# Attention with a learned bias and two MLP layers: query tiles moved to the outermost loop, heads taken two by two inside it

## The chip, the cores and the metric

The kernel runs on one core of a Trainium2 chip. The metric is the device time of one execution in microseconds (us); the time quoted for the kernel before is the median of 3 runs. A traced execution gives, beside its own time, a span from its first to its last instruction.

## What is computed

The reference works in float32 on a batch of 2, with 8 heads, a sequence of 576 and a head width of 64. Each score gets a bias that a small network computes from the distance of the two positions; the softmaxed scores weigh `v`; the result goes, token by token, through two gated MLP layers (hidden width 1536).

```python
scores = q @ k.T / sqrt(64)                               # B=2, H=8, S=576, D=64
x = log1p(abs(i - j)) / log1p(max(i, 1))                  # one number per (i, j)
bias = relu(x * w1 + b1) @ w2                             # 32 hidden units -> 8 heads
attn = softmax(scores + bias)
x = (attn @ v) as [1152 tokens, 512]
x = ((x @ w_a) * (x @ w_b)) @ w_out                       # first MLP, 512 -> 1536 -> 512
out = (silu(x @ w_gate) * (x @ w_val)) @ w2_out           # second MLP
```

## The kernel before

The 8 heads are handled as 4 pairs `p`. The 576 queries of a batch element are cut into tiles `t`: four of 128 rows (`t` = 0 to 3) and one of 64 (`t` = 4, for which the 64 rows of both batch elements share one tile of 128 partitions).

**Bias.** The bias depends on heads and positions, not on the batch, and is made once, in 36 units of 16 query rows for all heads. `Bias.make` runs four `hidden` operations (L122 on VectorE or L124 on ScalarE), fp32 matmuls (L146, 8 or 16 records each unit) and two to four scaling copies into a staging tile `bt` (L128, L130; `BTS` = 4 such tiles), which a DMA writes to a DRAM buffer `bias_d` (L159). A tile step reads its rows back (L349, or L353 and L354 into `pad` for `t` = 4). The first 12 units (`FIRST`) are made ahead of the first step, the others inside the first ten steps (`MADE`).

**Steps.** There are 20 steps (p, g, t). Group g = 0 holds the tiles 4, 0, 1 of a pair and g = 1 the tiles 2, 3. `Heads.load` fetches q of the group and the whole k of the pair for each (p, g), so that k is loaded and split into a high and a low part (`ka`, `kb`, L174 or L172 and L176) twice for each pair; `load_v` fetches v twice as well. Loads for the next (p, g) are put on SP's queue behind the bias reads of the current step. A step of a 128-row tile does, for each batch element b, one `scores` call: 12 matmuls into the four-bank PSUM tile `ps` (L256, one buffer), and for each head j a VectorE operation that adds the bias and finds the maximum (L259) and the exponential on ScalarE (L265). `es` is one tile for each head j with both batch elements side by side, from a ring of three. Then 18 transposes (L281) in groups of three go through a ring of three PSUM banks, each group copied to `ee` by VectorE or ScalarE (L271, L273, chosen by `Share`).

**Finish.** When the last tile of a (p, g) is done, `finish` turns the sums into reciprocals, spreads and transposes them (L295, L300, L303), multiplies `ee` with `v` for all 320 or 256 queries of one batch element at once (L312: 10 matmuls, each two records in the trace, into the one PSUM bank `pu`), scales (L314) and splits the result into `xh` and `xl` (L324, L325), the input of the MLPs.

**MLPs.** `moe` works on three chunks of 384 tokens. Its matmuls (L414) are 72 steps of 36. Weights come packed in pieces of 512 KB (`Weights.part`, L216 to L226); the first three pieces are asked for in step (2, 1, 2), the 17th of 20. The order of all instructions on each engine is set when the program is built, by a planner that goes by priorities in program order and its own costs.

Of the kernel before, what the change touches and what calls it, by code (L numbers as in the profile page):

```python
# [17 lines left out]
P = 128  # L18
# [10 lines left out]
QW = (704, 512)  # L29
LEFT = (512, 576)  # L30
TILES = ((4, 0, 1), (2, 3))
BW = 591
FAR = -1.0e30

UNITS = (*range(32, 36), *range(32))
FIRST = 12
MADE = (4, 4, 2, 2, 2, 2, 2, 2, 2, 2)
HDS, BTS = 8, 4
# [55 lines left out]
class Bias:  # L94
# [7 lines left out]
    def __init__(self, tc, stack, cst, lm, bias_d, heads, share):  # L102
# [15 lines left out]
        with tc.issue_after(ready.ins), tc.issue_after(last_load.ins):  # L118
            heads.load(0, 0)
# [12 lines left out]
    def make(self, u, banks):  # L132
# [9 lines left out]
        ps = [banks() for a in range(parts)]  # L142
        bt = self.bc.tile([P, BW], F32, tag="bt", name="bt", bufs=BTS)
        for a in range(parts):
            for cg in range(4):
                nc.tensor.matmul(ps[a][32 * cg : 32 * cg + 32, :w], self.W2, hd[cg][:, w * a : w * a + w], start=True, stop=True)  # L146
            if n == f:
                self.scaled(bt[:, z + w * a : z + w * a + w], ps[a][:, :w], w, u)
                c = min(z, w * a + w - 1) - max(w * a - 1, 0)
                if c > 0:  # L150
                    o = max(w * a - 1, 0)
                    self.scaled(bt[:, :z][:, ::-1][:, o : o + c], ps[a][:, 1 + o - w * a : 1 + o - w * a + c], c, u)
            else:
                self.scaled(bt[:, : z + 1][:, ::-1][:, w * a : w * a + w], ps[a][:, :w], w, u)
                c = min(f - 1, w * a + w - 1) - max(w * a - 1, 0)
                if c > 0:
                    o = max(w * a - 1, 0)
                    self.scaled(bt[:, z + 1 + o : z + 1 + o + c], ps[a][:, 1 + o - w * a : 1 + o - w * a + c], c, u)
# [3 lines left out]
class Heads:  # L162
# [5 lines left out]
    def split(self, raw, n, tags, bufs):  # L168
        hi, lo = (self.pool.tile([P, n[1]], F32R, tag=x, name=x, bufs=bufs) for x in tags)
        w = n[0]  # L170
        if self.share.on_dve(w, DFAST):
            self.nc.vector.tensor_copy(hi[:, :w], raw[:, :w])  # L172
        else:
            self.nc.scalar.copy(hi[:, :w], raw[:, :w])  # L174
        self.share.dve(w)
        self.nc.vector.tensor_tensor(lo[:, :w], raw[:, :w], hi[:, :w].bitcast(F32), op=ALU.subtract)  # L176
        return hi, lo

    def load(self, p, g):
        nc, n = self.nc, QW[g]  # L180
        raw = self.pool.tile([P, QW[0]], F32, tag="raw", name="raw", bufs=1)
        nc.sync.dma_start(raw[:, :n], self.d[0][p][:, g * QW[0] : g * QW[0] + n])
        kr = self.pool.tile([P, B * S], F32, tag="kr", name="kr", bufs=1)
        nc.sync.dma_start(kr, self.d[1][p])
        self.got["q", p, g] = self.split(raw, (n, QW[0]), ("qa", "qb"), 2)
        self.got["k", p, g] = self.split(kr, (B * S, B * S), ("ka", "kb"), 2)

    def load_v(self, p, g):
        vv = self.pool.tile([P, 2, 10, D], F32, tag="vv", name="vv", bufs=2)
        self.nc.sync.dma_start(vv, self.d[2][p])  # L190
        self.got["v", p, g] = vv
# [37 lines left out]
def attention(ctx, tc, a4, heads, share, bias, units, bias_d, xh, xl, weights, ident):  # L229
    nc = tc.nc  # L230
    with (
        tc.tile_pool(name="ac", bufs=1, reuse_waits="tile") as cpool,
# [5 lines left out]
        sums = cpool.tile([P, H, 9], F32, name="sums")  # L238
# [5 lines left out]
        pad = [cpool.tile([P, 640], F32, name=f"pad{i}") for i in range(2)]  # L244
        for x in pad:
            nc.vector.memset(x[:64, S:], FAR)
            nc.vector.memset(x[64:, :64], FAR)

        def scores(p, i, ops, n, es, bt):

            ps = ps2.tile([P, 2, 2, 512], F32, tag="big", name="ps")
            for hf in range(2):
                for m, (lt, rt) in enumerate(ops):
                    for j in range(2):
                        r = slice(64 * j, 64 * j + 64)
                        nc.tensor.matmul(ps[:, j, hf, :n], lt[r], rt[r, n * hf : n * hf + n], start=m == 0, stop=m == len(ops) - 1)  # L256
            for j in range(2):
                nm = a4.tile([P, 1], F32, tag="nm", name="nm")
                nc.vector.tensor_tensor_reduce(  # L259
                    out=es[j].rearrange("p (a j) -> p a j", a=2), in0=ps[:, j, :, :n], in1=bt[j].rearrange("p (a j) -> p a j", a=2),  # L260
                    op0=ALU.add, op1=ALU.min, scale=-0.125, scalar=3.0e38, accum_out=nm,
                )
                share.dve(2 * n, 1.3)
                share.act(2 * n, 190.0)
                nc.scalar.activation(es[j], es[j], AF.Exp, bias=nm, scale=-1.0, accum_out=sums[:, 2 * p + j, i : i + 1])  # L265

        ends = [None, None]

        def keep(dst, src):
            if share.on_dve(dst.free_size() if hasattr(dst, "free_size") else 384):  # L270
# [7 lines left out]
        def transposed(es, chunks):  # L278
            tp = bank()[:, : 3 * P].rearrange("p (k q) -> p k q", k=3)
            for n, kc in enumerate(chunks):  # L280
                nc.tensor.transpose(tp[:, n], es[:, P * kc : P * kc + P], ident)  # L281
            return tp

        def finish(p, g, ee):
            ts = slice(2 * g, 2 * g + 2)
            n = 256 if g else 320
            rs = a2.tile([P, 2, 5], F32, tag="rs", name="rs")
            nt = 4 if g else 5
            both = sums[:, 2 * p : 2 * p + 2]
            nc.vector.tensor_scalar_add(rs[:, :, :4].rearrange("p h (b t) -> p h b t", b=B), both[:, :, :8].rearrange("p h (b t) -> p h b t", b=B)[:, :, :, ts], 1e-9)  # L290
            if not g:
                nc.vector.tensor_scalar_add(rs[:, :, 4:], both[:, :, 8:], 1e-9)
            nc.vector.reciprocal(rs[:, :, :nt], rs[:, :, :nt])
            rw = a2.tile([P, 5, P], F32, tag="rw", name="rw", bufs=1)
            nc.scalar.copy(rw[:, :nt].rearrange("p i (h c) -> p i h c", h=2), rs[:, :, :nt].rearrange("p h i -> p i h").unsqueeze(3).to_broadcast([P, nt, 2, 64]))  # L295
            vv = heads.got["v", p, g]
            for b in range(B):
                rb = bank()
                for t in range(2):
                    nc.tensor.transpose(rb[:, P * t : P * t + P], rw[:, 2 * b + t], ident)  # L300
                if not g:
                    lb = slice(64 * b, 64 * b + 64)
                    nc.tensor.transpose(rb[:, 256:320], rw[lb, 4], ident[lb, lb])  # L303
                rc = a2.tile([P, 320], F32, tag="rc", name="rc", bufs=1)
                if share.on_dve(n):
                    nc.vector.tensor_copy(rc[:, :n], rb[:, :n])
                else:
                    nc.scalar.copy(rc[:, :n], rb[:, :n])
                pu = ps0.tile([P, 512], F32, tag="pu", name="pu")
                for kc in range(5):  # L310
                    for j in range(2):
                        nc.tensor.matmul(pu[64 * j : 64 * j + 64, :n], vv[:, j, 5 * b + kc], ee[:, j, 4 * b + kc, :n], start=kc == 0, stop=kc == 4)  # L312
                t1 = a2.tile([P, 320], F32, tag="t1", name="t1", bufs=2)
                nc.vector.tensor_tensor(t1[:, :n], pu[:, :n], rc[:, :n], op=ALU.mult)  # L314
                share.dve(n)
                share.dve(n)
                share.act(n)
                s0 = place(b, g)
                for c in range(NCH):
                    a, e = max(s0, CH * c), min(s0 + n, CH * c + CH)  # L320
                    if a < e:
                        dh = xh[c][:, p, a - CH * c : e - CH * c]
                        src = t1[:, a - s0 : e - s0]
                        nc.scalar.copy(dh, src)  # L324
                        nc.vector.tensor_tensor(xl[c][:, p, a - CH * c : e - CH * c], src, dh.bitcast(F32), op=ALU.subtract)  # L325
# [3 lines left out]
        lag = units.last  # L329
        rest = list(UNITS[FIRST:])  # L330
        after = {(0, 0): (1, 0), (1, 0): (2, 0), (2, 0): (3, 0), (3, 0): (0, 1), (0, 1): (1, 1), (1, 1): (2, 1), (2, 1): (3, 1)}
        steps = [(0, 0, 4), (1, 0, 4), (0, 0, 0), (1, 0, 0), (0, 0, 1), (1, 0, 1)]
        steps += [(p, 0, t) for p in (2, 3) for t in TILES[0]] + [(p, 1, t) for p in range(4) for t in TILES[1]]
        ee = {}
        for idx, (p, g, t) in enumerate(steps):
            if idx < len(MADE):
                for _ in range(MADE[idx]):
                    units.make(rest.pop(0), bank)
                if not rest:
                    bias.close()  # L340
                    weights.pool = ctx.enter_context(tc.tile_pool(name="wpa2", bufs=1, side="right"))
# [202 lines left out]
```

## Time and profile before

| | us |
|---|---|
| median of 3 runs | 701.7 (701.48 to 703.87) |
| the profiled execution | 702.97 |
| its span | 701.2 |
| first L259 of a 128-row tile begins | 54.88 |
| last L259 of the attention ends | 237.23 |

Engines: PE is TensorE's matmuls, PEld its weight loads, DVE is VectorE, ACT ScalarE, POOL GpSimd, SP the engine that issues all DMAs here. A busy PE is modelled from pipelined matmuls, so its share says less than the pace of its instructions.

### The profile page before, as it was taken

To read this page: it belongs to the slowest core of one execution; us is meant where nothing else is said; L and a number is where in the kernel's file an instruction comes from. 1 tells how busy PE (TensorE), PEld (TensorE's weight loads), DVE (VectorE), ACT (ScalarE), POOL (GpSimd) and SP (SyncE) were. 2 spreads that over 40 slices of the span, in tenths; PEclk is the share of its full clock that TensorE was granted. 3 is DMA by queue.
4 is the path that set the end of the run, shared out by engine and by line. 5 is a ranking of instruction groups with operands and counts; after the bars stand their busy time and mean duration, and the time that the engine had idled before them with its cause. 6 is when DMAs were issued, how large, how long until landed. Compare 5 with 4: busy or idle time off the path is not lost.

```text
span 701.2 us, 10805 instructions
## 1 busy us (share of the span) xinstructions
PE 647.1 (92%) x4112; PEld 565.8 (81%) x4112; DVE 458.2 (65%) x1006; ACT 326.4 (47%) x671; POOL 13.9 (2%) x19
## 2 busy tenths in 40 slices
PE   6665889897989989999999999999999999999997
PEld 3132555554656779999999999999999999999997
DVE  7664987955778489999949951299914982341222
ACT  6454775855658357445425431365514641221110
POOL 0000000000000000000000010202000000000000
PEclk9966999998989999999999999999999999999999
DMA  4775456534475034434423420033500530000111
GB/s 132 218 234 193 138 160 194 168 95 142 137 245 165 1 116 125 150 121 150 127 84 121 150 91 1 0 121 121 180 32 11 170 121 1 0 1 1 46 36 55
DMA packets 26516, 76.35 MB, mean 109 GB/s; under 512 B 2656, under 2 KB 4320, under 8 KB 26464
## 3 DMA queue, kind: packets, MB, share of 16 engines
q1 hardware_dynamic: 26464, 75.66, 34.3%
q8 instruction: 32, 0.52, 0.3%
q14 instruction: 20, 0.16, 0.1%
HBM read 62.40 MB, written 13.25 MB: 108 GB/s over the span
## 4 chain that ended last, share of the span: by engine, by line
PE 70%; DVE 4%; DMA 2%; ACT 1%; issue 1%; SPq 0%; DVEq 0%; ACTq 0%
PE p L414 43%; PE po L414 21%; PE pu L312 3%; PE tp L281 2%; PE ps L256 1%; DVE es L259 1%; DMA kr<-in_kd 1%; DMA raw<-in_wm 1%; DVE ee L271 1%; ACT es L265 0%; DVE kb L176 0%; DVE wl L226 0%; PE tp L300 0%; DVE acc L465 0%; DVE t L314 0%
## 5 line engine op out<-in xcount | busy, mean ns | idle before, releaser
L435 DVE TENSOR_TENSOR g<-p,g 128x384 f32<-128x384 f32 x72 | 40.0, 555 | 135.6 <-PE p L414 135.4
L414 PE MATMUL p<-xh,wh 128*128 128x384 f32 x288 | 96.5, 336 | 2.4 <-ACT g L434 1.6
L414 PE MATMUL p<-xh,wl 128*128 128x384 f32 x288 | 96.5, 335 | 0.0
L414 PE MATMUL po<-gh,wl 128*128 128x384 f32 x288 | 96.5, 335 | 0.0
L414 PE MATMUL p<-xl,wh 128*128 128x384 f32 x288 | 96.4, 335 | 0.0
L414 PE MATMUL p<-yh,wl 128*128 128x384 f32 x288 | 96.4, 335 | 0.0
L414 PE MATMUL po<-gl,wh 128*128 128x384 f32 x288 | 96.4, 335 | 0.0
L414 PE MATMUL p<-yh,wh 128*128 128x384 f32 x288 | 96.3, 335 | 0.0
L414 PE MATMUL p<-yl,wh 128*128 128x384 f32 x288 | 96.3, 334 | 0.0
L414 PE MATMUL po<-gh,wh 128*128 128x384 f32 x288 | 95.9, 335 | 0.0
L434 ACT ACTIVATE g<-p 128x384 f32<-128x384 f32 x72 | 35.3, 492 | 113.8 <-PE p L414 113.3
L281 PE MATMUL tp<-ident,es 128*128 128x128 f32 x328 | 56.1, 305 | 23.9 <-DVE bt L128 9.8
L437 ACT CAST gh<-g 128x384 fp32r<-128x384 f32 x72 | 37.0, 514 | 88.0 <-DVE g L435 87.9
L281 PEld LDWEIGHTS tp<-ident,es 128*128 128x128 f32 x328 | 38.8, 152 | 44.9 <-DVE bt L128 11.2
L219 ACT ACTIVATE m<-raw 128x512 f32<-128x512 f32 x72 | 48.2, 677 | 31.5 <-DVE wl L226 27.4
L265 ACT ACTIVATE es<-es,nm 128x576 f32<-128x576 f32 (+1 forms) x72 | 56.0, 778 | 10.0 <-DVE nm L259 9.5
L225 ACT CAST wh<-m 128x512 fp32r<-128x512 f32 x72 | 44.3, 620 | 33.2 <-DVE m L224 29.5
L414 PEld LDWEIGHTS p<-xh,wh 128*128 128x128 f32 x288 | 54.0, 188 | 3.5 <-ACT g L434 2.0
L146 PE MATMUL tp<-hd,cs 128*32 128x264 f32 (+17 forms) x352 | 43.4, 537 | 14.4 <-DVE hd L122 6.9
L414 PEld LDWEIGHTS p<-xh,wl 128*128 128x128 f32 x288 | 54.1, 188 | 0.4 <-issue 0.4
L414 PEld LDWEIGHTS p<-yl,wh 128*128 128x128 f32 x288 | 54.1, 188 | 0.0
L414 PEld LDWEIGHTS p<-xl,wh 128*128 128x128 f32 x288 | 54.1, 188 | 0.0
(67 smaller groups left out, 1123.9 us busy)
## 6 DMA issues: line engine op xcount, KB each, us to landing
raw<-in_wm SPq DMA_DIRECT2D x72, 512.0 KB
bias_d<-bt SPq DMA_DIRECT2D x36, 295.5 KB
bt<-bias_d SPq DMA_DIRECT2D x32, 288.0 KB
vv<-in_vd SPq DMA_DIRECT2D x8, 640.0 KB
kr<-in_kd SPq DMA_DIRECT2D x8, 576.0 KB
pad<-bias_d SPq DMA_DIRECT2D x16, 144.0 KB
out_t<-acc SPq DMA_DIRECT2D x12, 192.0 KB
raw<-in_qd SPq DMA_DIRECT2D x4, 352.0 KB
```

The lines of the kernel that those rows point to most:

```text
L146: nc.tensor.matmul(ps[a][32 * cg : 32 * cg + 32, :w], self.W2, hd[cg][:, w * a : w * a + w], start=True, stop=True)
L219: nc.scalar.activation(m, hi.bitcast(F32), AF.Abs)
L225: nc.scalar.copy(wh[:, i], m)
L256: nc.tensor.matmul(ps[:, j, hf, :n], lt[r], rt[r, n * hf : n * hf + n], start=m == 0, stop=m == len(ops) - 1)
L259: nc.vector.tensor_tensor_reduce(out=es[j].rearrange("p (a j) -> p a j", a=2), in0=ps[:, j, :, :n], in1=bt[j].rearrange("p (a j) -> p a j" ...
L265: nc.scalar.activation(es[j], es[j], AF.Exp, bias=nm, scale=-1.0, accum_out=sums[:, 2 * p + j, i : i + 1])
L281: nc.tensor.transpose(tp[:, n], es[:, P * kc : P * kc + P], ident)
L312: nc.tensor.matmul(pu[64 * j : 64 * j + 64, :n], vv[:, j, 5 * b + kc], ee[:, j, 4 * b + kc, :n], start=kc == 0, stop=kc == 4)
L414: nc.tensor.matmul(ps, lt, rt, start=first and n == 0, stop=last and n == len(parts) - 1)
L434: nc.scalar.activation(g, pp[0], AF.Silu if layer else AF.Copy)
L435: nc.vector.tensor_tensor(g, pp[1], g, op=ALU.mult)
L437: nc.scalar.copy(gh, g)
```

## The change

- Steps are (t, p) with the tile outermost, in the order 4, 0, 1, 2, 3, and the four pairs inside. k (split) and v of all four pairs stay on chip: each is loaded once, during the four steps of tile 4. q is loaded for each step alone (192 or 256 columns).
- A 128-row step consists of two half steps, one for each batch element. A half step makes its scores, transposes them at once (`es` now holds both heads of one batch element, ring of three; `ee` is 9 x 128 columns, ring of four) and multiplies with v at once, in 10 matmuls (20 records) of 128 columns. `finish` runs at the end of every step, 20 times and no longer 8 times.
- Tile 4 is done with 576 keys and two accumulating row blocks, with no padding; its 9 transposes and 3 copies replace 10 and 8.
- 4 bias units are made first, the other 32 over 17 half steps: 3 in each of the first four, then 2 and 1 in turn, and 2. `hd` has 6 buffers and no longer 8.
- The first pieces of the MLP weights are asked for in the 19th step.

```diff
-QW = (704, 512)
-TILES = ((4, 0, 1), (2, 3))
+ORDER = (4, 0, 1, 2, 3)
-FIRST = 12
-MADE = (4, 4, 2, 2, 2, 2, 2, 2, 2, 2)
-HDS, BTS = 8, 4
+FIRST = 4
+MADE = (3, 3, 3, 3, *(2, 1) * 6, 2)
+HDS, BTS, EES = 6, 4, 4
...
+    def load_q(self, p, t):
+        s, n = (0, 192) if t == 4 else (192 + 256 * t, 256)
+        raw = self.pool.tile([P, n], F32, tag=f"rawq{n}", name="rawq", bufs=1 if t == 4 else 2)
+        self.nc.sync.dma_start(raw, self.d[0][p][:, s : s + n])
+        self.got["q", p, t] = self.split(raw, (f"qa{n}", f"qb{n}"), 2)
...
+        self.got["k", p] = self.split(kr, (f"ka{p}", f"kb{p}"), 1)
...
+        vv = self.pool.tile([P, B, 10, D], F32, tag=f"vv{p}", name="vv", bufs=1)
...
+        def transposed(es):
+            ee = a2.tile([P, 9, P], F32, tag="ee", name="ee", bufs=EES)
+            for k in range(3):
+                tp = bank()[:, : 3 * P].rearrange("p (k q) -> p k q", k=3)
+                for n in range(3):
+                    o = P * (3 * k + n)
+                    nc.tensor.transpose(tp[:, n], es[:, o : o + P], ident)
+                keep(ee[:, 3 * k : 3 * k + 3], tp, 3 * P)
+            return ee
+
+        def values(p, pu, ee, blocks):
+            vv = heads.got["v", p]
+            for cols, b, o in blocks:
+                n = cols.stop - cols.start
+                for kc in range(5):
+                    for j in range(2):
+                        nc.tensor.matmul(pu[64 * j : 64 * j + 64, o : o + n], vv[:, b, 5 * j + kc], ee[:, 4 * j + kc, cols], start=kc == 0, stop=kc == 4)
...
+        steps = [(p, t) for t in ORDER for p in range(H // 2)]
...
+            with tc.issue_after(load.ins):
+                if idx + 1 < len(steps):
+                    if t == ORDER[0] and p < H // 2 - 1:
+                        heads.load_k(p + 1)
+                    heads.load_q(*steps[idx + 1])
+                    if t == ORDER[0] and p < H // 2 - 1:
+                        heads.load_v(p + 1)
+                if idx == len(steps) - 2:
+                    weights.load(3)
...
+                for b in range(B):
+                    make()
+                    es = scores(p, q, [(P * b, b)], bt, sums[:, 2 * b : 2 * b + 2])
+                    values(p, pu, transposed(es), [(slice(0, P), b, P * b)])
...
+            finish(p, t, pu, sums)
```

## Rows read from the trace of the kernel before

**Rows 1.** Page, part 4: the chain that ended last, by line.

```profile
PE p L414 43%; PE po L414 21%; PE pu L312 3%; PE tp L281 2%; PE ps L256 1%; DVE es L259 1%; DMA kr<-in_kd 1%; DMA raw<-in_wm 1%; DVE ee L271 1%; ACT es L265 0%; DVE kb L176 0%; DVE wl L226 0%; PE tp L300 0%; DVE acc L465 0%; DVE t L314 0%
```

**Rows 2.** Stretches of the attention: length, busy us and instructions, clock, DMA share, GB/s.

```profile
core 0: us, PE busy (x) PEld busy (x) DVE busy (x) ACT busy (x) POOL busy (x), PEclk, DMA share, GB/s
0.00:54.88 54.88, 35.05 (x266) 15.98 (x270) 36.31 (x94) 30.62 (x57) 0.74 (x7) 0.86 0.65 196
54.88:74.64 19.76, 12.08 (x88) 5.87 (x80) 12.00 (x37) 10.78 (x28) 0.00 (x0) 0.70 0.51 161
74.64:139.87 65.23, 58.03 (x477) 34.22 (x475) 55.63 (x146) 48.50 (x111) 0.00 (x0) 0.97 0.58 172
139.87:206.43 66.56, 55.51 (x406) 35.96 (x405) 42.31 (x106) 39.00 (x93) 0.00 (x0) 0.90 0.48 155
```

**Rows 3.** The same stretches, L259 alone: each addition is two records.

```profile
74.64:139.87 65.23, 18.00 (x48) 0.97 0.58 172
139.87:206.43 66.56, 17.79 (x49) 0.90 0.48 155
206.43:237.23 30.80, 11.90 (x32) 1.00 0.37 112
```

**Rows 4.** One stretch, matmuls of the bias units (L146) alone.

```profile
74.64:139.87 65.23, 9.77 (x96) 2.20 (x96) 0.97 0.58 172
```

**Rows 5.** Waits of the first 75 us: who waited for whom, us, times, longest.

```profile
ACT bt L130 <- DMA bias_d<-bt: 17.9, 6, 5.1
```

**Rows 6.** Waits from 139.87 to 206.43 us, in the same form.

```profile
DVE t L314 <- PE pu L312: 10.9, 6, 2.2
...
ACT qa L174 <- DMA raw<-in_qd: 3.9, 1, 3.9
```

**Rows 7.** Windows of the start, all engines: columns as in the stretches.

```profile
0.00:17.50 17.50, 11.40 (x115) 5.50 (x119) 13.01 (x33) 12.03 (x20) 0.74 (x7) 1.00 0.44 131
17.50:35.00 17.50, 10.55 (x77) 3.46 (x72) 11.62 (x33) 7.69 (x15) 0.00 (x0) 0.93 0.74 219
35.00:52.50 17.50, 10.73 (x66) 5.25 (x62) 11.20 (x31) 10.44 (x22) 0.00 (x0) 0.70 0.77 232
...
25.00:30.00 5.00, 2.52 (x14) 0.55 (x8) 2.01 (x6) 2.27 (x4) 0.00 (x0) 1.00 0.96 273
```

**Rows 8.** DMA issues of the whole span: operands, times issued, KB of each.

```profile
bias_d<-bt SPq DMA_DIRECT2D x36, 295.5 KB
...
vv<-in_vd SPq DMA_DIRECT2D x8, 640.0 KB
kr<-in_kd SPq DMA_DIRECT2D x8, 576.0 KB
pad<-bias_d SPq DMA_DIRECT2D x16, 144.0 KB
```

**Rows 9.** Pieces of the chain that ended last: start us, us, what.

```profile
153.79 8.07 DMA kr<-in_kd
...
175.35 2.87 PE pu L312 x20
...
190.83 7.95 DMA raw<-in_wm
...
214.80 2.31 PE pu L312 x20
...
222.01 1.02 PE tp L281 x8
...
234.76 0.99 PE ps L256 x12
```

**Rows 10.** Timeline of PE: start us, us, instruction, shape, count.

```profile
11.91 0.31 PE L256 MATMUL ps<-kb,qa 64*128 64x320 f32 x2
12.06 0.31 PE L256 MATMUL ps<-ka,qb 64*128 64x320 f32 x2
12.30 2.19 PE L146 MATMUL tp<-hd,cs 128*32 128x280 f32 x32
```

More of the change, by code (lines that the diff above doesn't have):

```diff
@@ L242, in bias_rows, with scores @@
             return bass.AP(tensor=e.tensor, offset=e.offset + 15, ap=[[16 * BW, n // 16], [BW - 1, 16], [1, S]])
[L244 to L249, printed above, removed]
+        ends = [None, None]
+        def scores(p, q, blocks, bt, sums):
+            ka, kb = heads.got["k", p]
+            qa, qb = q
             ps = ps2.tile([P, 2, 2, 512], F32, tag="big", name="ps")
+            es = a4.tile([P, 2, S], F32, tag="es", name="es", bufs=3)
@@ L262, in scores @@
                 )
[L263 to L270, printed above, removed]
+                share.dve(S, 1.3)
+                share.act(S, 190.0)
+                nc.scalar.activation(es[:, j], es[:, j], AF.Exp, bias=nm, scale=-1.0, accum_out=sums[:, j : j + 1])
@@ L271, in keep @@
+            return es.rearrange("p h k -> p (h k)")
+        def keep(dst, src, n):
+            if share.on_dve(n):
                 ends[1] = nc.vector.tensor_copy(dst, src)
@@ L276, in bank @@
             return ps1.tile([P, 512], F32, tag="tp", name="tp", bufs=3)
[L278 to L309, printed above, removed]
@@ L310, in finish @@
                 for kc in range(5):
                     for j in range(2):
[L312 to L318, printed above, removed]
@@ new lines, in finish @@
+        def finish(p, t, pu, sums):
+            s0, n = place(t)
+            nb = n // P
+            rs = a2.tile([P, 2 * nb, 1], F32, tag=f"rs{nb}", name="rs")
+            nc.vector.tensor_scalar_add(rs, sums.unsqueeze(2), 1e-9)
+            nc.vector.reciprocal(rs, rs)
+            rw = a2.tile([P, nb, P], F32, tag=f"rw{nb}", name="rw", bufs=1)
+            nc.scalar.copy(rw.rearrange("p b (h c) -> p (b h) c", h=2), rs.to_broadcast([P, 2 * nb, 64]))
+            rb = bank()
+            for b in range(nb):
+                nc.tensor.transpose(rb[:, P * b : P * b + P], rw[:, b], ident)
+            rc = a2.tile([P, 256], F32, tag="rc", name="rc", bufs=1)
+            if share.on_dve(n):
+                nc.vector.tensor_copy(rc[:, :n], rb[:, :n])
+            else:
+                nc.scalar.copy(rc[:, :n], rb[:, :n])
+            t1 = a2.tile([P, 256], F32, tag="t1", name="t1", bufs=2)
+            nc.vector.tensor_tensor(t1[:, :n], pu[:, :n], rc[:, :n], op=ALU.mult)
+            share.dve(n)
+            share.dve(n)
+            share.act(n)
+            share.act(n)
+            for c in range(NCH):
+                a, e = max(s0, CH * c), min(s0 + n, CH * c + CH)
+                if a < e:
+                    dh = xh[c][:, p, a - CH * c : e - CH * c]
+                    src = t1[:, a - s0 : e - s0]
+                    nc.scalar.copy(dh, src)
+                    nc.vector.tensor_tensor(xl[c][:, p, a - CH * c : e - CH * c], src, dh.bitcast(F32), op=ALU.subtract)
@@ L389, in attention, with make @@
-    return ends
-def place(b, g):
-    return 640 + 256 * b if g else 320 * b
+        steps = [(p, t) for t in ORDER for p in range(H // 2)]
+        half = 0
+        def make():
+            nonlocal half
+            for _ in range(MADE[half] if half < len(MADE) else 0):
+                if rest:
+                    units.make(rest.pop(0), bank)
+                    if not rest:
+                        bias.close()
+                        weights.pool = ctx.enter_context(tc.tile_pool(name="wpa2", bufs=1, side="right"))
+            half += 1
@@ L397, in moe, with place @@
+    return ends
+def place(t):
+    return (0, P) if t == 4 else (P + 2 * P * t, 2 * P)
 def moe(tc, xpool, xh, xl, weights, out, ends):
@@ L478, in moe, with token_rows @@
             project(*p)
+def token_rows():
+    rows = [None] * NT
+    for t in ORDER:
+        s, n = place(t)
+        rows[s : s + n] = [S * b + P * t + r for b in range(B) for r in range(n // 2)]
+    return rows
 def kernel(**inputs):
@@ L522 @@
     arrays = {
-        "qd": qd.reshape(H // 2, P, sum(QW)),
-        "kd": kd.reshape(H // 2, P, B * S),
-        "vd": vd.reshape(H // 2, 2, P, 10, D).transpose(0, 2, 1, 3, 4).reshape(H // 2, P, 20 * D),
+        "qd": qd.reshape(H // 2, P, 64 + NT),
+        "kd": kt.reshape(H // 2, P, NT),
+        "vd": vd,
         "cst": np.concatenate([w1c, b1c, w2c.reshape(P, 32), ps, re_], axis=1),
@@ L537 @@
     r = run_bass_kernel_spmd(nc, [arrays], core_ids=[0])
-    rows = r.results[0]["out_t"].T
-    out = np.empty((B, S, DM), np.float32)
-    for b in range(B):
-        x, y = place(b, 0), place(b, 1)
-        out[b, :256], out[b, 512:], out[b, 256:512] = rows[x : x + 256], rows[x + 256 : x + 320], rows[y : y + 256]
-    return out.reshape(NT, DM)
+    out = np.empty((NT, DM), np.float32)
+    out[rows] = r.results[0]["out_t"].T
+    return out
```

155 lines of the change are left out of this document (50 added, 105 removed).

## The prediction

> **What bounds the kernel now.** I read the chain that ended last first. Two thirds of it are MLP matmuls [rows 1], which the diff doesn't touch; the last addition of a bias (L259) ends at 237.23 us and everything behind it takes 464 us in both kernels. So the question is when the attention ends. For that I cut its span at the starts of additions and asked for busy times and counts.
>
> The reader is to see four stages in [rows 2, 3]. The first, to 54.88 us, is that of the early units and the first two steps of tile 4: TensorE, VectorE and ScalarE are busy for 35, 36 and 31 of 55 us, while the DMA engines reach a share of 0.74 to 0.77 [rows 7] and 0.96 in one window of 5 us. ScalarE alone waits 17.9 us for staging tiles whose write to `bias_d` hasn't landed [rows 5]. This stage is bound by transfers. The third stage (74.64 to 139.87) holds 24 additions, which is 5 wide steps and 2 of tile 4, and 12 bias units (96 records of 8) [rows 3, 4]. The fourth (139.87 to 206.43) holds 24 additions, 6 wide steps and little else, and yet takes 66.56 us, 11.1 for each step, with VectorE at 42 and ScalarE at 39 us. The last (206.43 to 237.23) does 4 wide steps in 30.8 us, 7.7 each [rows 3].
>
> What the fourth stage waits for is in [rows 6, 9]: the chain runs through 8.07 us of a second load of k, ScalarE waits 3.9 us for q with it, the first MLP weights stand in the chain with 7.95 us, and VectorE waits 10.9 us in 6 waits for the long value blocks of `finish`.
>
> What a wide step costs when nothing is late can be added up for TensorE from [rows 9]: two scores blocks at 0.99 are 1.98 us; 18 transposes at 1.02/8 = 0.1275 are 2.30; 20 value records of 256 columns are 2.31; two more transposes for the reciprocals are 0.26. That is 6.85 of the 7.7 us. In [rows 10] a change from one kind of matmul to the next takes 0.24 us from start to start where the pair before it came 0.15 behind its predecessor, so about 0.09 is paid at each change, and some eight changes a step make up most of what is left. In a plain step TensorE's own instruction stream is the bound.
>
> **The change part by part.** *First stage.* Up to the additions of the fourth tile-4 step the new kernel must move, by the sizes in [rows 8]: 12 units at 295.5 KB (3.55 MB; of the 16 that are made in this stage the last four are needed later), 16 reads of 144 KB (2.3), k four times 576 KB (2.3), v four times 640 KB (2.56), the two tables (0.4), and q four times 96 KB (192 columns of 128 rows, 0.38): 11.5 MB. Before, the first 17.5 us move 131 GB/s or 2.3 MB, and I leave that, since the units and k come first here too. The other 9.2 MB go at the mean of the two windows that follow, 225 GB/s [rows 7], in 41 us: the first wide addition comes at 58.5 us. Bounds: 273 GB/s, the best window, gives 51 us; 161 GB/s, the rate of the second stretch [rows 2], gives 75. So this stage is no shorter than before, but it leaves less behind: all four steps of tile 4 are done with it, where before two of them came in the third stage; 16 wide steps and 20 units remain.
>
> New waits on SP's queue: the load of k for the next pair needs the single `kr` buffer, hence the split of the last k (L174, L176), and behind it stand the writes of bias units and the next bias reads. What waits for these is again ScalarE and VectorE for staging tiles. It is inside the DMA-bound stage and costs nothing beyond the bound above.
>
> *Wide steps.* Scores, additions, exponentials, transposes and copies keep their number and size. `finish` comes every step with 256 columns in place of every second step with two batch elements: per step the same scalings and splits as in the last stretch, so nothing on top of 7.7. The second load and split of k, and the wait for it, go: with k there from the first stage, the middle steps run at the pace of the last ones. q comes in pieces of 128 KB one step ahead; the step before covers it, and without that cover it is the 3.9 us of [rows 6].
>
> The value matmuls are what gets dearer. A wide step now has 40 records of 128 columns for 20 of 256. The price of a short one is not in the trace. From below: 2.87/20 = 143.5 ns at 320 columns and 2.31/20 = 115.5 at 256 give 0.4375 ns a column and 59.5 ns at 128, that is 2.38 us a step and no change. From above: a transpose, also 128 columns but with twice the weight columns to load, takes 127.5 ns; 40 of these are 5.1 us, 2.8 more. The nearest row is the bias unit's matmul, fp32 in column groups like this one: 32 in 2.19 us, 68 ns [rows 10], the closest spacing of fp32 matmuls with their own weights in these rows. I take 68: 2.72 us, 0.41 more. One more value block a step is two more changes of kind at 0.09: 0.18. So 7.7 + 0.41 + 0.18 = 8.3 us.
>
> The Trainium skill, page "TensorE: Matmul & The Clock Gate", section "Back-to-back issue gap", gives about 81 ns for a stream of weight load and matmul pairs at 128 columns. By that the 640 records of the wide steps cost 13 ns more each than in my sum, 8.3 us in all, and the time would be 696. Another page of the skill, "TensorEngine Tiling (Array Packing)", section "Tiling Modes", says that a change of tiling mode drains TensorE, which speaks against cutting the values into more blocks; the 0.09 us above agrees in kind.
>
> *Bias units.* From the third stage: 65.23 less 5 x 7.7 less 2 steps of tile 4 at half a wide one (7.7) leaves 19.0 for 12 units, 1.6 each; with tile-4 steps at 5.5 it is 1.3. I take 1.5. The nearest bounds: TensorE alone needs 8 x 0.068 = 0.55 of it.
>
> *MLP weights.* They are asked for two steps later. Before, the request stood in the chain for 7.95 us but the MLP began only when the attention's scores were done. In the new order the request goes out some three steps (25 us) before the end. Between 0 and 8 us; I take 2, because no k load competes with it any more.
>
> *Tile 4*: its padding, two small copies a head and one transpose go; inside the DMA-bound stage this is worth nothing. `hd` with 6 buffers holds one and a half units; ScalarE and VectorE, not this ring, limit a unit, so nothing.
>
> Sum: 58.5 + 16 x 8.3 + 20 x 1.5 = 221.3 us for the end of the last addition, against 237.23: 15.9 earlier. Less 2 for the weights, 13.9. On the profiled execution's own 702.97 that is 689.1; the median stands 1.3 lower, so 688.
>
> **The rivals.** *Short value matmuls wait for their weights.* Place: the 32 value blocks of the wide steps. For it: a transpose, whose columns are as few, already runs at 127.5 ns and not at 59.5; TensorE is the bound there, so every ns counts in full. Against it: the bias matmuls at 68, though with half as many weight columns. At 127.5 ns the wide steps cost 640 x 0.0595 = 38 us more: 726. It decides from 68 + 13.9/0.64 = 90 ns on; above that the kernel is slower.
>
> *The middle steps stay slow.* The fourth stage lost 66.56 - 6 x 7.7 = 20 us. If that was not k but the value blocks and the copies of `finish` (10.9 us of waits in [rows 6]), and 20 finishes bring it back, half of it gives 698 and all of it 708.
>
> *A longer first stage.* k and v of all pairs are now wanted at the start, where the queue is full already. At 161 GB/s the first wide step comes at 75 us, 16 later: 704, no change.
>
> *Units for nothing.* If TensorE bounds the steps with units as well, a unit costs its 0.55 us and no more, since VectorE and ScalarE have room beside it; half steps with an `es` for each leave the planner more to choose from. 20 x 0.95 = 19 us less: 670. Against it: the third stage, where a unit cost 1.3 to 1.6 with VectorE busy for 55.6 of 65.2 us.
>
> **How the numbers follow.** The forecast's own range is 680 to 696, with a chance of 0.42. Units for nothing: 0.17, faster. Middle steps slow: 0.14, of which 0.06 is still faster, 0.04 the same, 0.04 slower. Longer first stage: 0.11, 0.07 of it the same and 0.04 slower. Short value matmuls past 90 ns: 0.16, slower. Together: faster by over 0.5% (below 698.2; half a per cent is about what a measurement of this kernel can tell from no change) 0.65, within it 0.11, slower 0.24. The range goes from 670, the unit rival's time, to 707, which leaves out some 0.13 above and 0.07 below; it holds the DMA bound (704) and a value record up to 97 ns.
>
> **What would show it.** First wide addition near 58 us, with all eight tile-4 additions ahead of it; no wait for `kr` after that. Steps without units 8 to 8.5 us from addition to addition, those with three units about 12.5. Value blocks of 20 records in 1.2 to 1.5 us. The last addition near 221. The forecast is wrong if value records stand 90 ns apart or more, if a wide step without units takes 10 us, or if the first wide addition comes after 70 us.

## The result and the profile after

The change makes the kernel slower: 708.2 us (median of 5 runs, 707.1 to 709.5) against 701.5 (5 runs beside them), a ratio of 1.009 with a 95% interval of 1.0067 to 1.0113. The profiled execution took 708.51 us, its span 706.7. On record stood 688, range 670 to 707.

The page's chain by line, which answers to [rows 1]: MLP matmuls (L404) as before, but two loads that weren't in it or hardly, q and k, now hold 3% of the span each.

```profile
PE p L404 42%; PE po L404 21%; PE pu L299 6%; PE tp L146 5%; PE tp L288 5%; PE ps L259 4%; DMA rawq<-in_qd 3%; DMA kr<-in_kd 3%; DMA raw<-in_wm 1%; DMA bias_d<-bt 1%; PE tp L311 1%; DVE es L264 1%; DVE hd L122 1%; ACT es L270 1%; DMA LW<-in_lm 0%
```

Stretches of the attention in the form of [rows 2], cut where the first wide addition begins (81.45), where the first step without units begins (175.99) and just behind the end of the last addition (244.03; it ends at 243.92):

```profile
0.00:81.45 81.45, 52.03 (x449) 28.16 (x449) 41.88 (x104) 36.45 (x76) 0.73 (x7) 0.83 0.54 157
81.45:175.99 94.54, 88.71 (x802) 51.85 (x803) 76.60 (x216) 65.99 (x157) 0.00 (x0) 0.98 0.49 137
175.99:244.03 68.04, 66.14 (x682) 49.95 (x683) 55.09 (x154) 44.93 (x115) 0.00 (x0) 1.00 0.40 120
```

The additions alone (L264, two records each; compare [rows 3]):

```profile
0.00:81.45 81.45, 5.92 (x16) 0.83 0.54 157
81.45:175.99 94.54, 23.20 (x64) 0.98 0.49 137
175.99:244.03 68.04, 23.17 (x64) 1.00 0.40 120
```

The 8 additions of tile 4 (16 records) are spread over 81 us in which no engine is busy for more than 52. Behind that come 8 wide steps with 20 units in 94.5 us and 8 plain ones in 68.0, 8.5 each, or 8.1 without the 3.5 us by which the step with the MLP weights is longer than its neighbours. From the first wide addition to the end of the last one it is 162.5 us; the prediction's own terms give 16 x 8.3 + 20 x 1.5 = 162.8, or 164.8 with its 2 us for the weights. The miss lies in the first stage, and that is 23 us longer: 81.45 in place of 58.5.

What the first stage waits for, in pieces of the chain that ended last (start, length, what) and, below, in its waits up to 82 us:

```profile
18.53 2.99 DMA bias_d<-bt
...
24.09 9.69 DMA kr<-in_kd
...
35.99 11.15 DMA kr<-in_kd
...
48.28 9.59 DMA rawq<-in_qd
...
62.24 5.47 DMA rawq<-in_qd
...
79.91 7.34 DMA rawq<-in_qd
```

```profile
ACT qa L174 <- DMA rawq<-in_qd: 16.4, 2, 10.8
...
DVE es L264 <- DMA bt<-bias_d: 10.6, 3, 5.5
...
DVE ka L172 <- DMA kr<-in_kd: 8.6, 3, 7.6
```

A load of 576 KB takes 10 to 11 us from issue to landing and one of 96 KB nearly 10. The split behind such a load stands in ScalarE's and VectorE's streams, and what is behind the split stands still with it. One would expect the DMA engines to be full meanwhile. They are for a part of the time only. Here are 40 slices of one us from 20 to 60 us, busy share in tenths and GB/s, of the changed kernel:

```profile
DMA  8001298999999522389989622257976887522222
GB/s 236 5 7 14 94 164 295 280 268 247 243 327 390 204 108 97 104 231 325 250 217 252 165 92 108 104 129 268 323 199 150 289 251 213 204 120 94 102 100 100
```

Again and again the share falls to 0.2 and the rate to about 100 GB/s, while loads are outstanding. Those are the stretches in which nothing is left but reads of `bias_d` for tile 4 and the last parts of the transfers behind them. The trace's semaphore events tell why. A load of k, q or v posts 16 of them, a 128-row read of bias rows 9, a read for tile 4 only 5 (the changed kernel; the number ahead of the colon is the us of the issue, those behind it the us of each event):

```
L355 bt<-bias_d   23.37:  24.5, 31.9, 32.0, 32.3, 32.5
L187 kr<-in_kd    24.09:  28.2, 28.4, 28.4, 28.5, 28.5, 28.7, 28.8, 28.8, 28.9, 28.9, 29.1, 29.2, 33.2, 33.3, 33.6, 33.8
L187 kr<-in_kd    35.99:  40.0, 40.0, 40.1, 40.1, 40.1, 40.2, 40.2, 40.2, 40.3, 40.4, 40.4, 40.4, 46.4, 46.5, 46.8, 47.1
L352 bt<-bias_d   79.27:  80.3, 86.7, 86.8, 86.8, 86.9, 86.9, 86.9, 87.0, 87.1
L182 rawq<-in_qd  79.91:  83.1, 83.2, 83.2, 83.3, 83.3, 83.4, 83.4, 83.5, 87.0, 87.0, 87.2, 87.2, 87.2, 87.2, 87.2, 87.2
```

The Trainium skill, page "DMA: Bandwidth & Descriptors", section "Why a DMA increments its semaphore by 16 and not by 1", says that a transfer spreads over the largest number of engines up to 16 that divides the slowest dimension of both sides, the lowest-numbered ones, and that the issuing queue posts the rest of the 16 at once. This trace agrees: `bias_rows` reads with the pattern `[[16 * BW, n // 16], [BW - 1, 16], [1, S]]`, whose slowest dimension is 4 for the 64 rows of tile 4 and 8 for 128 rows; 5 and 9 events are 4 and 8 with the one jump ahead of them, and a digit of 2, a share from 0.2 to 0.3, holds 4 of 16 engines (0.25). The loads behind them say the same: of k's 16 parts 12 land by 40.4 and four at 46.4 to 47.1, and of the q that stands behind 128-row reads eight land by 83.5 and eight at 87.0 to 87.2. A load has 16 parts, and the engines that the narrow reads have kept busy are late with theirs. Which engines these are by number, no row here tells. Before, the same narrow reads were there, but two of the four tile-4 steps came later; the change puts all 16 of them, and the k, q and v of all pairs behind them, into the first stage.

### The profile page after: what moved, and what is told of

Its sections match the earlier page's. It is cut to its first block, busy times and chain, and to the rows that moved or that the text cites. A ratio compares the mean times of both kernels' runs of the same rounds, so it can differ in the third digit from the quotient of the medians.

```text
span 706.7 us, 11756 instructions
## 1 busy us (share of the span) xinstructions
PE 663.4 (94%) x4584; PEld 584.3 (83%) x4584; DVE 460.4 (65%) x1034; ACT 322.4 (46%) x675; POOL 13.9 (2%) x19
## 4 chain that ended last, share of the span: by engine, by line
PE 83%; DMA 8%; DVE 4%; ACT 2%; issue 2%; SPq 1%; DVEq 0%; ACTq 0%
PE p L404 42%; PE po L404 21%; PE pu L299 6%; PE tp L146 5%; PE tp L288 5%; PE ps L259 4%; DMA rawq<-in_qd 3%; DMA kr<-in_kd 3%; DMA raw<-in_wm 1%; DMA bias_d<-bt 1%; PE tp L311 1%; DVE es L264 1%; DVE hd L122 1%; ACT es L270 1%; DMA LW<-in_lm 0%
## 5 line engine op out<-in xcount | busy, mean ns | idle before, releaser
L404 PE MATMUL p<-xh,wh 128*128 128x384 f32 x288 | 96.7, 336 | 2.2 <-ACT g L424 2.2
L404 PE MATMUL p<-xl,wh 128*128 128x384 f32 x288 | 96.5, 335 | 0.0
L404 PE MATMUL po<-gh,wl 128*128 128x384 f32 x288 | 96.5, 335 | 0.0
L404 PE MATMUL p<-xh,wl 128*128 128x384 f32 x288 | 96.4, 335 | 0.0
L404 PE MATMUL p<-yh,wl 128*128 128x384 f32 x288 | 96.4, 335 | 0.0
L404 PE MATMUL p<-yh,wh 128*128 128x384 f32 x288 | 96.3, 335 | 0.0
L404 PE MATMUL po<-gl,wh 128*128 128x384 f32 x288 | 96.3, 335 | 0.0
L404 PE MATMUL p<-yl,wh 128*128 128x384 f32 x288 | 96.3, 334 | 0.0
L404 PE MATMUL po<-gh,wh 128*128 128x384 f32 x288 | 95.9, 335 | 0.0
L288 PE MATMUL tp<-ident,es 128*128 128x128 f32 x324 | 56.0, 294 | 15.3 <-ACT es L270 14.3
L146 PE MATMUL tp<-hd,cs 128*32 128x264 f32 (+17 forms) x352 | 54.2, 525 | 15.0 <-DVE hd L122 8.3
L288 PEld LDWEIGHTS tp<-ident,es 128*128 128x128 f32 x324 | 35.1, 144 | 39.5 <-issue 18.5
L299 PE MATMUL pu<-ee,vv 128*64 128x128 f32 (+1 forms) x800 | 65.2, 274 | 2.1 <-ACT ee L277 1.8
L270 ACT ACTIVATE es<-es,nm 128x576 f32<-128x576 f32 x72 | 55.5, 771 | 23.5 <-DVE nm L264 22.9
L299 PEld LDWEIGHTS pu<-ee,vv 128*64 128x64 f32 x800 | 45.8, 138 | 22.9 <-issue 9.5
L264 DVE CUSTOM_DVE_ANT_0 es<-ps,bt 128x576 f32<-128x576 f32 x72 | 51.9, 752 | 13.0 <-DMA bt<-bias_d 11.7
L404 PEld LDWEIGHTS p<-xh,wh 128*128 128x128 f32 x288 | 54.1, 188 | 2.5 <-ACT g L424 2.5
```

The costliest lines, as they stand in the source:

```text
L146: nc.tensor.matmul(ps[32 * cg : 32 * cg + 32, :w], self.W2, hd[cg][:, w * a : w * a + w], start=True, stop=True)
L264: nc.vector.tensor_tensor_reduce(out=es[:, j].rearrange("p (a j) -> p a j", a=2), in0=ps[:, j, :, :288], in1=bt[j].rearrange("p (a j) -> p ...
L270: nc.scalar.activation(es[:, j], es[:, j], AF.Exp, bias=nm, scale=-1.0, accum_out=sums[:, j : j + 1])
L288: nc.tensor.transpose(tp[:, n], es[:, o : o + P], ident)
L299: nc.tensor.matmul(pu[64 * j : 64 * j + 64, o : o + n], vv[:, b, 5 * j + kc], ee[:, 4 * j + kc, cols], start=kc == 0, stop=kc == 4)
L404: nc.tensor.matmul(ps, lt, rt, start=first and n == 0, stop=last and n == len(parts) - 1)
```

## The experiments

All times are medians beside runs of the kernel before on the same chip; ratios are to it. "First wide" is the start of the first addition of a 128-row step (81.45 in the changed kernel).

**1 and 2. Bias reads on all 16 engines.** The rows within a query tile are taken in another order (q and the output are permuted to match, outside the kernel), so that 16 can be the slowest dimension. In the first kernel for tile 4 alone, in the second for all tiles. Bytes, number of transfers and instructions stay, and VectorE, ScalarE and SP have their instructions in the same order as in the changed kernel.

```diff
-ap=[[16 * BW, n // 16], [BW - 1, 16], [1, S]]
+ap=[[BW - 1, 16], [16 * BW, n // 16], [1, S]]
...
+        m = n // 32
+        order = [16 * (x % m) + x // m for x in range(n // 2)]
```

> Only the order of the 64 rows within tile 4 is changed (on the host and in the read's access pattern), so that the 16-row dimension comes first in each of tile 4's bias reads. Theory A, that these 16 reads run on only four of the sixteen DMA engines and everything behind them waits for those four: the first wide addition moves from 81 to about 60 to 66 us and the time falls by 13 to 20 us, to 688 to 695. Theory B, that the loop of one raw k buffer (load, split, next load) sets the first stage: no more than 4 us. Theory C, that the stage is bound by the total of bytes: nothing.

Measured: 695.3 us, ratio 0.9895 (0.9872 to 0.9919), first wide at 66.5. Time and place lie just past the slow ends of the first theory's ranges and far from the other two's.

> The same for the reads of all tiles. Theory A: as with tile 4 alone, and up to 3 us more, since the 128-row reads run on eight engines now but are covered by the step before. Theories B and C: as there, at most 4 us.

Measured: 690.2 us, ratio 0.9817 (0.9792 to 0.9843), first wide at 65.5. The slices of the second kernel in the same 40 us, and its chain:

```profile
DMA  0067979989999879999999997856088900018209
GB/s 28 0 157 203 258 205 338 262 234 358 401 388 374 201 256 384 346 384 338 289 305 316 398 345 265 237 194 196 2 142 280 303 12 0 0 28 210 76 5 217
```

```profile
24.57 7.33 DMA vv<-in_vd
31.96 5.30 DMA kr<-in_kd
...
38.41 5.74 DMA rawq<-in_qd
...
64.12 4.49 DMA rawq<-in_qd
```

The long stretches at a share of 0.2 are gone, k lands 5.3 us after its issue and no longer 11, and ScalarE's wait for q falls from 16.4 to 8.2 us. The size fits too. An estimate from these rows: 16 reads of 144 KB, 2.36 MB, take 23.6 us at 100 GB/s and 7.8 at the 302 that this kernel moves from 32 to 48 us, a difference of 15.8; the first wide addition came 15.0 earlier by tile 4 alone. The wide tiles' reads (8 engines) were worth 5 more by the medians and 3 in the profiled executions, 1 of it before the first wide addition.

**3. More buffers for the loads.** The rival: it is the single buffer of k and of tile 4's q that makes loads late.

```diff
-        raw = self.pool.tile([P, n], F32, tag=f"rawq{n}", name="rawq", bufs=1 if t == 4 else 2)
+        raw = self.pool.tile([P, n], F32, tag=f"rawq{n}", name="rawq", bufs=2)
...
-        kr = self.pool.tile([P, B * S], F32, tag="kr", name="kr", bufs=1)
+        kr = self.pool.tile([P, B * S], F32, tag="kr", name="kr", bufs=2)
```

> Two raw buffers for k and for tile 4's q, nothing else. Theory B: the next k is asked for before the last one is split, so each of the three tile-4 steps behind the first loses 3 to 4 us of about 12, the first wide addition comes at about 70 us, the time falls by 8 to 12 us. Theory A: the same four engines stay full, 0 to 3 us. Theory C: nothing.

Measured: 716.3 us, ratio 1.0189 (1.0158 to 1.0219), first wide at 87.1: 8 us slower than the changed kernel. No theory had that, and the rival gets no support; against it speaks kernel 2, which gains 16 us in the first stage with the single buffers. A clean test of the buffers this is not: with room for a second load the planner put a split of k ahead of two additions that it stood behind (L172 at 57.46, the additions at 58.91 and 60.25; in the changed kernel they start at 52.65 and 54.41, and the split at 59.36). VectorE now waits 14.3 us in front of k's splits and no longer 8.6:

```profile
ACT qa L174 <- DMA rawq<-in_qd: 17.2, 2, 10.5
...
DVE ka L172 <- DMA kr<-in_kd: 14.3, 4, 6.8
```

**4. Value matmuls twice.** The price of the short records was the prediction's largest unknown. Each block of values is multiplied twice over; the second accumulation starts over, so the sums in `pu` stay what they were.

```diff
-                for kc in range(5):
+                for kc in (*range(5), *range(5)):
```

> The value matmuls of every half step are done twice (the second accumulation starts over, so the values are the same). If TensorE bounds the wide steps, the time grows by the price of 640 records of 128 columns: 37 us at 58 ns, 43 us at 68 ns. If the wide steps wait for VectorE or ScalarE, it grows by less than 20 us.

Measured: 754.6 us, ratio 1.0736 (1.0702 to 1.0769), 46.4 more than the changed kernel. The expectation counted the 640 records of the wide steps; the edit adds 800, with the 160 of tile 4, which have 64 columns. That is 58 ns for each of the 800, or 72 if those of tile 4 were free; they were not quite, the first wide addition came 5 us later. TensorE's stream does bound the wide steps. In the chain, blocks of the doubled kernel run at 63 ns a record. Those of the changed kernel run at 58 in one block of 40, at 62 and 71 in two blocks of 20, and at 80 in blocks of ten, of which the chain has most; first a line of the doubled kernel, then the changed one's, with its request for MLP weights:

```profile
153.68 1.89 PE pu L299 x30
```

```profile
198.00 1.24 PE pu L299 x20
...
202.43 0.80 PE pu L299 x10
...
216.01 6.89 DMA raw<-in_wm
...
241.50 2.33 PE pu L299 x40
```

**5. The same repair in the kernel before.** What is the change worth where no read is narrow?

```diff
-ap=[[16 * BW, n // 16], [BW - 1, 16], [1, S]]
+ap=[[BW - 1, 16], [16 * BW, n // 16], [1, S]]
...
+    rows_of = [P * t + 16 * (x % m) + x // m for t in range(5) for m in (8 if t < 4 else 4,) for x in range(16 * m)]
+    qt = a("q").transpose(1, 3, 0, 2)[..., rows_of]
```

> The kernel before, with the rows of every query tile taken in another order so that each read of bias rows has 16 as its slowest dimension (16 engines) and no longer 8 or 4; nothing else changes. Theory A, any load queued behind a read that uses few engines lands late: the second loads of k and q in the middle steps (8.07 and 3.9 us of the chain and the waits) come earlier, and the kernel before gains 4 to 10 us: 693 to 698. Then the change itself, both with spread reads (690.2 for the changed kernel), is worth 3 to 8 us. Theory B, only the bunching of all 16 reads of tile 4 in the first stage makes them hurt: the kernel before stays within 2 us of 702, and the change with spread reads is worth 12.

Measured: 690.3 us, ratio 0.982 (0.9797 to 0.9842). Both kernels with wide reads take the same time, 690.3 and 690.2: the change by itself is worth nothing that these runs can tell from zero. Neither theory had that; the second fell, and the first had the gain (11.6 us, more than expected) in the wrong place. The second load of k in the middle still stands in the chain for 9.09 us, where it was 8.07 [rows 9]. The stretches of this kernel, cut at the same additions as [rows 2], the second and third of those rows in one, and then those of kernel 2, cut like the changed one above:

```profile
0.00:47.60 47.60, 34.77 (x278) 15.20 (x278) 36.18 (x95) 31.12 (x58) 0.73 (x7) 0.93 0.72 225
47.60:126.40 78.80, 68.07 (x551) 39.00 (x547) 67.32 (x182) 58.94 (x136) 0.00 (x0) 0.94 0.63 184
126.40:192.70 66.30, 55.27 (x422) 35.77 (x423) 42.28 (x105) 39.48 (x94) 0.00 (x0) 0.95 0.50 156
192.70:223.50 30.80, 26.49 (x224) 18.01 (x220) 25.63 (x68) 22.29 (x54) 0.00 (x0) 1.00 0.35 111
```

```profile
0.00:65.50 65.50, 48.60 (x449) 27.05 (x449) 41.51 (x104) 36.36 (x76) 0.73 (x7) 0.90 0.66 198
65.50:157.10 91.60, 87.38 (x802) 51.01 (x803) 76.27 (x217) 65.49 (x157) 0.00 (x0) 1.00 0.51 141
157.10:224.30 67.20, 65.87 (x681) 49.68 (x681) 54.75 (x154) 44.74 (x114) 0.00 (x0) 1.00 0.41 118
```

In the kernel before the first three stretches get 13.5 us shorter (54.88 to 47.6, 84.99 to 78.8) and the last two, 66.3 and 30.8, don't move. The changed kernel then has the faster steps (158.8 us from its first wide addition to the end of the last, with 20 units inside, where the kernel before takes 175.9 with two steps of tile 4 and its own units), and pays for them in its first stage, 65.5 against 47.6. That cancels: the last addition ends at 224.4 and 223.5.

**6. MLP weights asked for two steps earlier**, on top of kernel 2.

```diff
-                if idx == len(steps) - 2:
+                if idx == len(steps) - 4:
```

> The changed kernel with all reads of bias rows on 16 engines (690.2 us), and the first three pieces of the MLP weights asked for two steps earlier. Theory A: the late request costs the 4 us by which the step around it is longer than its neighbours; asked for early, they come while nothing else is loaded and the time is 686 to 687. Theory B: the step is longer because the preparation of the weights takes VectorE and ScalarE from the step, wherever it stands: 689 to 691.

Measured: 689.1 us, ratio 0.9807 (0.9782 to 0.9832). The 1.1 us are inside the intervals, so the time decides nothing by itself (see 11). The long step moves with the request and stays long: it takes 11.2 us from 182.7 to 193.9 where kernel 2 has 11.4 from 198.5 to 209.9, which is what the second theory says.

**7. Splits behind the step**, on top of kernel 2: a load is issued where it was, its split is emitted behind `finish`.

```diff
-        self.got["k", p] = self.split(kr, (f"ka{p}", f"kb{p}"), 1)
+        self.due.append((("k", p), kr, (f"ka{p}", f"kb{p}"), 1))
...
             finish(p, t, pu, sums)
+            heads.settle()
```

> The changed kernel with all reads on 16 engines (690.2 us), with the splits of k and q emitted behind the work of the step in which their loads are issued, and not ahead of it. Theory A: what is left of the first stage beyond the forecast (65.5 against 58.5 us) is VectorE and ScalarE standing in front of a split whose load has not landed; then the first wide addition comes at 60 to 62 us and the time is 685 to 687. Theory B: the splits are themselves on the way to the next step, and putting them later gives nothing or costs: first wide addition at 65 us or later, 690 or more.

Measured: 686.8 us, ratio 0.9775 (0.976 to 0.9789), first wide at 64.2. The time is the first theory's, the place neither's: only 1.3 of the 3.4 us were gained ahead of the first wide addition.

**8. Fewer bytes**, on top of kernel 2: v of the first pair serves all pairs; three loads of 640 KB are left out.

```diff
+        if p:
+            self.got["v", p] = self.got["v", 0]
+            return
```

> The changed kernel with all reads on 16 engines (690.2 us), v loaded for the first pair alone and used for all four (three loads of 640 KB left out, so the output is that of another v). Theory A: the bytes bound what is left of the first stage; 1.9 MB less at 225 GB/s is 8.5 us, the first wide addition at 57 us and the time 682. Theory B: order and latency bound it, not bytes: the first wide addition moves by less than 2 us and the time stays at 688 to 691.

Measured: 694.7 us, ratio 0.9887 (0.9871 to 0.9904), first wide at 68.9: later, with less to move, which neither theory had. From 32 to 48 us this kernel moves 142 GB/s where kernel 2 moves 302:

```profile
32.00:48.00 16.00, 10.33 (x91) 6.48 (x91) 9.23 (x20) 3.44 (x9) 0.00 (x0) 0.71 0.46 142
```

The last k landed earlier, at 42.2 us and not at 45.5, and the first wide addition still came later. With three loads fewer the planner laid out the other work differently: from 33.6 us on, VectorE has another order of instructions. So the run shows that fewer bytes don't suffice for a shorter stage; what the bytes alone are worth, it does not show.

**9. The loads on another queue**, reads left narrow: k, q and v go through GpSimd's queue.

```diff
-        self.nc.sync.dma_start(kr, self.d[1][p])
+        self.nc.gpsimd.dma_start(kr, self.d[1][p])
```

> The changed kernel with its reads of bias rows left on 4 and 8 engines, and the loads of k, q and v put on GpSimd's DMA queue, away from SP's, where the reads stand. Theory A, a load is late because it stands behind the narrow reads in the same queue: on a queue of its own it lands earlier, the first wide addition comes at 65 to 72 us in place of 81.5, and the time is 692 to 699. Theory B, the few engines that the narrow reads use are themselves the backlog, whatever queue a load comes from: first wide addition at 78 us or later, 705 to 712.

Measured: 699.1 us, ratio 0.9963 (0.9948 to 0.9977), first wide at 74.9. Between the two. The loads are also issued earlier: all of v by 4.5 us, and the second to fourth k at 8.5, 20.5 and 29.8 where the changed kernel has 24.1, 36.0 and 49.5. Behind 20 us they no longer stand in the chain, and the narrow reads themselves do, with a share of 0.2 for most of the time from 36 to 54 us (its chain behind 20 us, and its slices from 20 to 60 us):

```profile
30.09 9.87 DMA bt<-bias_d
...
69.63 5.26 DMA bt<-bias_d
```

```profile
DMA  0669981000169998222275222222223224829426
GB/s 29 65 184 307 387 312 42 14 0 12 60 161 247 249 282 312 116 94 97 97 221 205 104 101 93 95 103 97 104 101 118 101 106 144 264 116 257 172 102 181
```

It gave 9 of the 18 us of kernel 2, and the reads stay narrow. That a queue of its own frees a load is not shown: most loads were issued ahead of the reads, VectorE's and ScalarE's orders differ from the changed kernel's, and the one k that was issued among the reads (29.79) had twelve parts there by 35.5 and the last four at 37.5 to 38.3. For that load the second theory holds.

**10. Twelve units first**, on top of kernel 2.

```diff
-FIRST = 4
-MADE = (3, 3, 3, 3, *(2, 1) * 6, 2)
+FIRST = 12
+MADE = (1, 1, 1, 1, *(2, 1) * 6, 2)
```

> The changed kernel with all reads of bias rows on 16 engines (690.2 us), but 12 bias units made first, as in the kernel before, and one in each tile-4 step in place of three. Theory A: the units fill waits for transfers in the tile-4 steps, so that moving 8 of them ahead lengthens the first stage by 2 to 6 us: 692 to 696. Theory B: it is the units that hold up the tile-4 steps, and made first they cost less: 684 to 688.

Measured: 686.6 us, ratio 0.9793 (0.9761 to 0.9824). The time is the second theory's, the place isn't: the first wide addition came at 66.6, no earlier than in kernel 2, and the gain lies in the steps behind it. Why, stays open; the plan of those steps differs as well. The gain is 3.6 us by the medians and 1.7 by the ratios, whose intervals overlap, so it is not clear of noise.

**11 and 12. What helped, together.** Kernel 11 is 7 with the edit of 6; kernel 12 adds that of 10.

> All reads on 16 engines, splits behind the step (686.8 us), and the MLP weights asked for two steps earlier (1.1 us by itself, within its error). If the two gains are separate, 684.5 to 686.5; if both filled the same gaps, 686.5 to 688. Either way the fastest version here, against 690.3 for the kernel before with spread reads.

Measured: 684.0 us, ratio 0.9751 (0.9724 to 0.9777), the fastest here and just under the range for separate gains: 24 us under the changed kernel and 6 under the repaired kernel before, which was not run with these two changes. The earlier request is worth 2.8 us on top of the late splits by the medians and 1.7 by the ratios, whose intervals overlap.

> All edits that helped, together: all reads on 16 engines, splits behind the step, MLP weights asked for two steps earlier (684.0 us with these three), and 12 units made first with one in each tile-4 step (worth 3.6 us by itself). Theory A: the gains are separate, 680 to 681.5. Theory B: units made first and late splits fill the same gap, in which VectorE and ScalarE stood in front of late loads: 683 to 685.

Measured: 686.5 us, ratio 0.9778 (0.9745 to 0.9812). That is above both ranges and nearer the second's: units made first and late splits don't add up. Whether they cost something together is not shown, since the interval overlaps that of kernel 11.

## Why the prediction was wrong

*First stage: the step that failed.* It was priced as 11.5 MB at the mean rate of two windows of the kernel before, 225 GB/s. That took the DMA engines for one pipe. The rate belonged to a mixture, with eight of the narrow reads in it, and the change altered the mixture: 16 narrow reads in groups of four, three of the groups with loads of k, q and v behind them. With reads on 16 engines the stage takes 65.5 us, and with tile 4's alone 66.5, against 81.45. Of the 23 us of the miss 16 are the narrow reads.

The other 7 go with a second fault of the sum, its bytes. From 17.5 us to the first wide addition it has 9.2 MB at 225 GB/s. The changed kernel and then kernel 2 moved, in the same stretch:

```profile
17.50:81.45 63.95, 40.27 (x360) 21.85 (x357) 32.29 (x84) 26.99 (x61) 0.00 (x0) 0.79 0.56 163
```

```profile
17.50:65.50 48.00, 36.93 (x355) 21.07 (x353) 31.13 (x82) 26.01 (x59) 0.00 (x0) 0.86 0.72 219
```

That is 10.4 MB at 163 GB/s and 10.5 at 219. Kernel 2 has nearly the forecast's rate and 1.3 MB more, which at 219 GB/s is 6 us (an estimate from these rows). The sum had left out the bias reads and q of the wide steps, of which four and three were issued by then, and all units behind the twelfth, where 14 were issued. This is an account and not a cause: kernel 8 had fewer bytes and was later, in another order, and from 48 to 65.5 us kernel 2's engines have a share of 0.53. What sets these 7 us stays open; kernel 7 took away 1.3 of them by another order of the splits.

The hint stood in the trace of the kernel before. The stretch from 54.88 to 74.64, which gave the prediction its slow bound of 161 GB/s [rows 2], holds four of these reads, and in half-us slices from 50 to 70 us it looks like this:

```profile
DMA  3569998454545557983399598886322222106970
GB/s 96 187 211 243 332 407 293 171 166 152 195 187 212 206 199 260 285 333 153 144 229 305 205 267 296 282 282 225 154 103 94 113 99 80 57 38 156 222 265 14
```

From 64.5 to 67 us 0.2 of the engines move 80 to 113 GB/s. The writes of staging tiles for which ScalarE waited [rows 5], read by the prediction as a sign of full DMA engines, were late by as few: the one issued at 56.49 landed on its first engine at 59.21 and on its last at 65.80. The prediction took the slow bound as an unlikely end; at 163 GB/s it was what came. "A longer first stage", at 75 us and a chance of 0.11, was the right rival at the right rate. It had 75 us and not 81 because it too counted 9.2 MB for 10.4, and its reason was a full queue and not reads that use few engines.

*Wide steps: right, the record's price partly by luck.* 8.1 us in the plain steps for 8.3, the weights taken apart. In long blocks and in blocks of ten the value records cost 58 to 80 ns for the 68 taken, and no rival's 90 or more. But the row that gave the 68 [rows 10] is of matmuls with 280 columns in groups of 32 weight columns, so it is no price of a record of 128; that it lies inside the range is luck, while the 59.5 ns worked out from the longer records are close to what the block of 40 took. The 81 ns of the Trainium skill's page "TensorE: Matmul & The Clock Gate" ("Back-to-back issue gap") are met by the blocks of ten (80), which hold a change of kind, and not by the longer ones. The 696 us that go with 81 were missed for another reason, the first stage. Middle steps that stay slow: refuted. k is there, and the 162.5 us behind the first wide addition leave no room for it.

*Units: right.* With plain steps of 8.1 us, (94.54 - 8 x 8.1) / 20 = 1.5 us each, as forecast; with 8.5 it is 1.3. "Units for nothing" is refuted.

*MLP weights: mis-sized.* The step behind the request (it goes out at 216.0) took 12.0 us (217.4 to 229.4), 3.5 more than its neighbours, for the 2 in the sum. Asked for earlier it gives 1.1 to 2.8 back by the medians, neither clear of noise.

*The kernel before.* The prediction took its first stage as it stood. It too lost 11.6 us to the narrow reads, which kernel 5 shows, so most of what the repair gives isn't the change's. With wide reads on both sides, the change's steps are as cheap as forecast and its first stage is 18 us longer than the one it replaces, where 3.6 was forecast: that is where the gain of 14 us went.

## What to carry to other kernels

A mean rate of DMA windows is a price only for the mixture that made it. Before moving transfers together, look at slices of a microsecond: here a share that stood at a fixed low fraction while loads were outstanding meant transfers that use few engines, and their access pattern's slowest dimension said how many. Reordering rows so that this dimension is 16 cost no instruction here and gave 11.6 us to one kernel and 18 to the other, more than the whole restructuring of the loops. More buffers for loads and fewer bytes both made things slower here (by 8 and 4.5 us): each brought another order of the instructions with it, so neither run shows what the buffers or the bytes alone are worth.

## What the runs showed that was not expected

A load spread over 16 engines is as late as its busiest engine: behind reads on four of them, the last four parts of a load of k came 6 us after the other twelve. The same held on another queue, with a lag of 2 us, and the narrow reads went on at about 100 GB/s. And fp32 value records of 128 columns, 128 rows by 64 weight columns, ran at 58 ns apiece in a block of 40 (2.33 us), where a transpose of as many columns takes 127.5 [rows 9].
